# A mixture's first product as seven half-size products, its weights' sums streamed from DRAM

## The chip, the cores and the metric

One of the cores of a Trainium2 chip (trn2) runs the whole kernel. The metric is the device time of one execution in microseconds; lower is better. All data are fp32.

## The reference

A recurrence of attention kind (four batches, eight heads, 768 steps, head size 40) feeds a mixture of four experts:

```python
for t in range(S):
    y[:, :, t] = np.einsum('bhd,bhde->bhe', rt, state)
    Sa = np.einsum('bhde,bhe->bhd', state, at)
    state_decay = state * wt[:, :, None, :] - np.einsum('bhd,bhe->bhde', Sa, bt)
    state = state_decay + np.einsum('bhd,bhe->bhde', vt, kt)
x = y.transpose(0, 2, 1, 3).reshape(3072, 320)
p = domain_probs / (domain_probs.sum(-1, keepdims=True) + 1e-09)
for e in range(4):
    h = np.maximum(x @ w1[e], 0.0)            # 320 -> 1024
    out += p[:, e:e + 1] * (h @ w2[e])        # 1024 -> 320
```

## The kernel before, in words

**Units and chunks.** The 768 steps are cut into 12 chunks of 64. A unit is one chunk of two batches, 128 rows; there are 24 units, two to a chunk. The recurrence inside a unit is written in closed form: small products of 64x64 and 32x32 on PE (L371, L583, L595), a triangular system solved by substitution on POOL (L544, L557), and the state carried from unit to unit (L692, L693). The steps of a unit, by the names of their PSUM tiles: pg, pNT and pKT turn data; pc, pfe and pev are scores and their products (`within`); pY and pQ finish the triangular inverse (`merge`); prn, psat, pxr and pdy are the recurrent step (`step`). On DVE, ET and SX are masked copies (L382) of pfe and pxr; G is a running product (L401); `blocks` and M (L516, L519) prepare the substitution. pdy needs SX. Its result Y goes by twelve DMAs (L711) into xT, the transposed input of the mixture.

**The mixture.** From the second chunk on both units of a chunk go through the mixture together: 256 tokens, 320 inputs in two groups of 128 rows and a last one of 64. `up` (L718) makes one half of an expert's hidden layer from a piece of w1: 8 matmuls of 128 rows by 256 tokens (L734), and the last 64 inputs as 4 matmuls that take turns in the two halves of the array's rows (L726). Each fp32 matmul shows as two instructions in the trace. The result lies in two PSUM banks of the tag `mm`, which has three, and ACT writes relu of it to SBUF (L739). The second product, h times w2, is already done as seven half-size products for each expert: sums of w2 are made once (`add_weights`), sums of h by DVE after each expert (`add_h`, L835), and the products (L841) in `down_1` and `down_2`. DVE adds them into the output with the gates (L750, L752). The down products of an expert are issued while the next one's up products are.

**Order.** The main loop (L1021) runs the generators of three units side by side and calls `gap` four times for each unit; a gap puts two parts of the mixture (`mix`) onto the queues. The framework's scheduler may still move instructions within what dependences allow, except where `keep_in_program_order` pins them. Each engine then works through its compiled list. w1 is loaded anew for each chunk, in pieces of 512 KB and two times 64 KB (L282), into two buffers; a new load goes out when the piece before the last has been used (`used`). SP issues these loads, the loads of the next units (natW, natB, natK, natV at L184, the raw forms at L205), xT (L711) and the output (L757) from one queue. V is copied from natV into VC by ACT (L462).

Of the kernel before, what the change touches and what calls it, by code (L numbers as in the profile page):

```python
# [7 lines left out]
FP32 = mybir.dt.float32  # L8
I32 = mybir.dt.int32
ALU = mybir.AluOpType  # L10
ACTF = mybir.ActivationFunctionType
# [4 lines left out]
def kernel(  # L16
# [35 lines left out]

    nc = tc.nc

    B, H, S, D = r.shape
    E, DM, F = moe_w1.shape
    P = 128
    L = 64  # L60
    Q = 32
    NC = S // L
# [5 lines left out]
    const = ctx.enter_context(tc.tile_pool(name="const", bufs=1))  # L68
    sb = ctx.enter_context(tc.tile_pool(name="sb", bufs=1))
    ps = ctx.enter_context(tc.tile_pool(name="ps", bufs=1, space=bass.MemoryType.PSUM))  # L70

    def big(name):
        return ps.tile([P, 512], FP32, name=name, tag="big", bufs=5)
# [6 lines left out]
        base=0, channel_multiplier=-1,  # L80
    )

    upf = sb.tile([P, L], FP32, name="upf", tag="s", bufs=3)
    diagf = sb.tile([P, Q], FP32, name="diagf", tag="s", bufs=3)
    for t, n, op in ((upf, L, ALU.is_gt), (diagf, Q, ALU.is_equal)):
        nc.vector.memset(t[:], 1.0)
        for q in range(P // n):
# [26 lines left out]
    def set_pick():  # L114
        nc.gpsimd.memset(pick, 0.0)
        for n, (g, j) in enumerate(PLACES):
            for s in range(2):
                for c in (0, DT) if g == 2 else (0,):
                    w_ = DT if g == 2 else P
                    o = pick[64 * s:64 * s + D, n, c:c + w_]  # L120
                    nc.gpsimd.affine_select(
                        out=o, in_=o, pattern=[[-1, w_]], compare_op=ALU.not_equal, fill=1.0,
                        base=(2 * j + s) * D - g * P, channel_multiplier=1,
                    )

    first = const.tile([P, 2 * NJ, L], FP32, name="first")
    nc.gpsimd.memset(first[:], 0.0)
# [51 lines left out]

    def load(q, names):  # L180
        for x in names:
            q.n[x] = t = sb.tile([P, H, D], FP32, name=f"nat{x}", tag=f"nat{x}", bufs=2 if x in "WV" else 1)
            for i, bb in enumerate(q.b):
                nc.sync.dma_start(  # L184
                    out=t[i * L:(i + 1) * L], in_=srcs[x][bb, :, q.c * L:(q.c + 1) * L, :].rearrange("h t e -> t h e"),
                )
# [27 lines left out]
    def part(i):  # L214
        return slice(i * L, (i + 1) * L)
# [39 lines left out]
    class Piece:  # L255
        pass

    n_pieces = 2 * E * (1 + NC)
    pieces = []

    in_sums = {k + 5 * x: k - 1 for x in range(3) for k in (1, 2, 3)}
# [1 line left out]
    def load_piece():  # L263

        k = len(pieces)
        e, x = k // 2 % E, k % 2
        if k in in_sums:
            t = sums[in_sums[k]]
        else:
            t = sb.tile([P, PIECE], FP32, name="w1p", tag="w1p", bufs=2)  # L270
        q = Piece()
        q.main = t[:, 0:2 * HF * P].rearrange("p (g c) -> p g c", g=2)
        q.last = t[:, 2 * HF * P:PIECE].rearrange("p (f c) -> p f c", c=P)
        cols = slice(x * HF * P, (x + 1) * HF * P)
        moves = [(q.main, moe_w1[e, 0:2 * P, cols].rearrange("(g p) c -> p g c", p=P))]
        for i in range(2):
            half_cols = slice((2 * x + i) * HF // 2 * P, (2 * x + i + 1) * HF // 2 * P)
            moves.append(
                (q.last[i * DT:(i + 1) * DT], moe_w1[e, 2 * P:DM, half_cols].rearrange("d (f c) -> d f c", c=P))
            )  # L280
        for to, src in moves:
            tc.keep_in_program_order(nc.sync.dma_start(out=to, in_=src))  # L282
        pieces.append(q)

    def used(n):

        while len(pieces) < n_pieces:
            k = len(pieces)
            if k in in_sums:
                before = k - 5 if k >= 5 else -1  # L290
            else:
                at = [x for x in range(k) if x not in in_sums]
                before = at[-2] if len(at) > 1 else -1
            if before >= n:
                break
            load_piece()

    def load_w2(e):
        tc.keep_in_program_order(nc.sync.dma_start(out=w2_sb[e][:], in_=moe_w2[e].rearrange("(f p) d -> p f d", p=P)))
# [84 lines left out]
    def within(q):  # L384
# [24 lines left out]
        yield  # L409

        pg = by(turn("pg", tok(Gv), q.u == 2)[:], 64)[:, :, 0:D]
        gp = sb.tile([P, H, D], FP32, name="gp")
        pin(nc.vector.tensor_tensor(out=gp[:], in0=pg, in1=n["W"][:], op=ALU.mult))
        pin(nc.vector.reciprocal(out=gp[:], in_=gp[:]))  # L414

# [20 lines left out]
            nc.scalar.copy(out=t[:].rearrange("p j t -> p (j t)"), in_=turn("p" + name, tok(x), q.u == 1)[:])  # L436
            return t

        def token_V():
            return n["paddedV"][:, :, 0:D] if q.u < PADDED else n["V"][:]  # L440

        def causal_scores(VT):
            pc = quadrants(banks("pc"), 0, BY_TOKENS, L, lambda j, s, i: (
                d_half(j, s), i, j, of_slots(VT, d_half(j, s), j, i, D), of_slots(q.RT, d_half(j, s), j, i, D),
# [13 lines left out]
        ins = nc.vector.tensor_tensor(out=at_ij, in0=at_ij, in1=Gv.rearrange("p (j i) t -> p i j t", i=2), op=ALU.mult)  # L458
        pin(ins)
        q.VC = VCs()  # L460
        if q.u > 0:
            nc.scalar.copy(out=q.VC[:, :, 0:D], in_=token_V())  # L462
        if q.u >= PADDED:
            VT = turn_rv()
        yield
# [28 lines left out]
        yield  # L494

        if q.u == 0:
            tc.keep_in_program_order(nc.scalar.copy(out=q.VC[:, :, 0:D], in_=token_V()))
        q.EV = EVs()
        pev = quadrants(banks("pev"), 0, BY_TOKENS, D, lambda j, s, i: (
            i, i ^ s, j, ET[half(i), head(j, s), :], q.VC[half(i), head(j, s), 0:D],  # L500
# [9 lines left out]

    def substitute(q, eng, between=None):

        blocks = sb.tile([P, H, Q], FP32, name="blocks")
        for i in range(P // Q):
            move = nc.scalar.copy if i >= 2 else nc.vector.tensor_copy
            tc.keep_in_program_order(move(out=blocks[quarter(i)], in_=q.F[quarter(i), :, quarter(i % 2)]))  # L516
# [7 lines left out]
        on_diag = M[:].rearrange("p c r -> p (c r)")[:, Q + 1::2 * (Q + 1)]  # L524
        tc.keep_in_program_order(nc.vector.memset(on_diag, 0.0))

        Z = sb.tile([P, 4, Q // 4, Q], FP32, name="Z")
        q.Z = Z[:, 0]
        by_second = Z[:, 1:3].rearrange("p x k r -> p (x k) r")
        below = M[:].rearrange("p c r -> p (c r)")[:, 1::2 * (Q + 1)]  # L530
# [32 lines left out]
    def merge(q):  # L563


        Qc = sb.tile([P, H, Q], FP32, name="Qc", tag="q", bufs=2)
        QTc = sb.tile([P, H, Q], FP32, name="QTc", tag="q", bufs=2)
        tc.keep_in_program_order(nc.vector.transpose(out=dealt(Qc[:]), in_=q.Z))
        tc.keep_in_program_order(
            nc.vector.transpose(  # L570
                out=QTc[:].rearrange("p h r -> p (h r)"), in_=Qc[:].rearrange("p h c -> p (h c)"),
            )
        )
        q.QT = QTs()
        for i in range(P // Q):
            ins = nc.gpsimd.tensor_copy(out=q.QT[quarter(i), :, quarter(i % 2)], in_=QTc[quarter(i)])  # L576
            tc.keep_in_program_order(ins)
        yield

        py = big("pY")  # L580
        for h in range(H):
            for i in (1, 3):
                nc.tensor.matmul(  # L583
                    out=py[quarter(i - 1), h * Q:(h + 1) * Q], lhsT=q.F[quarter(i), h, 0:Q],
                    rhs=QTc[quarter(i), h, :], start=True, stop=True,
                )
        Y = sb.tile([P, H, Q], FP32, name="Yq")
        for i in (0, 2):
            nc.scalar.copy(out=Y[quarter(i)].rearrange("p h t -> p (h t)"), in_=py[quarter(i), 0:H * Q])
        yield  # L590

        pq = big("pQ")
        for h in range(H):
            for i in (0, 2):
                nc.tensor.matmul(  # L595
                    out=pq[quarter(i), h * Q:(h + 1) * Q], lhsT=Qc[quarter(i), h, :],
                    rhs=Y[quarter(i), h, :], start=True, stop=True,
                )
        for i in (0, 2):
            nc.scalar.copy(out=q.QT[quarter(i), :, quarter(1)], in_=by(pq[quarter(i), 0:H * Q], Q))  # L600
        yield
# [116 lines left out]
    def up(k, xT, n, width):  # L718

        w1 = pieces[k]  # L720
        h = sb.tile([P, HF, 2 * P], FP32, name="hs", tag="hs", bufs=3)
        ph = [ps.tile([P, HF // 2, n], FP32, name="ph", tag="mm", bufs=3) for _ in range(2)]

        for f in range(HF // 2):
# [90 lines left out]
    def mixture_of_chunk(qs, xT):  # L815

        hs, a_sums, osb = {}, {}, []
        at = 2 * E * (qs[0].c + 1)

        def ups(e, x):  # L820
            hs[e, x] = up(at + 2 * e + x, xT, 2 * P, P)
            used(at + 2 * e + x + 1)

        def of_h(e, s, x):
            return hs[e, x][:, :, s * P:(s + 1) * P]

        def add_h(e):
            a = {(s, x): of_h(e, s, x) for s in range(2) for x in range(2)}
            for n, x, y, op in (
                (1, a[0, 0], a[1, 1], ALU.add), (7, a[0, 1], a[1, 1], ALU.subtract),  # L830
                (5, a[0, 0], a[0, 1], ALU.add), (2, a[1, 0], a[1, 1], ALU.add),
                (6, a[1, 0], a[0, 0], ALU.subtract),
            ):
                t = a_sums[e, n] = sb.tile([P, HF, P], FP32, name=f"a{n}")
                nc.vector.tensor_tensor(out=t[:], in0=x, in1=y, op=op)  # L835
# [49 lines left out]


        before = last[:]
        for e in range(E):
            todo.append(lambda e=e: ups(e, 0))
            if before:  # L890
                todo.append(before[0])
                todo.append(lambda e=e: ups(e, 1))
                todo.append(lambda e=e, then=before[1]: (then(), add_h(e)))
            else:
                todo.append(lambda e=e: (ups(e, 1), add_h(e)))
            second = down_2_at_end if (qs[0].end and e == E - 1) else down_2
            before = [lambda e=e: down_1(e), lambda e=e, second=second: second(e)]
        last[:] = before
# [104 lines left out]
    run(m)  # L1003
    run(s, 2)
    run(ws[2], 1)
    load(units[3], "WBKV")
    go(load_raw(units[3], "AVR"))
    mix(1)
    run(ws[2], 3)
# [11 lines left out]
    for u in range(1, NU):  # L1021
# [32 lines left out]

        if u + 3 < NU:
            go(load_raw(begin(u + 3), "WA"))
            load(units[u + 3], "WBKV")
            later.extend(load_raw(units[u + 3], "VR"))
        run(w, 2)
        if early:  # L1060
# [58 lines left out]
```

## Time and profile before

| | |
|---|---|
| runs | 1143.93 and 1148.85 us, median 1146.39 |
| profiled execution | 1141.15 us, its span 1139.1 us |
| granted TensorE clock, mean | 0.988 |
| one unit in the steady part | 43.6 us |
| busy DVE, 600 to 700 us | 72.71 us |
| DMA read and written | 111.79 and 3.93 MB |

Rows of the timeline read: start, length, engine, line, operation, output <- inputs, shapes (array rows x columns, then partitions x elements), how many instructions are merged, and in brackets the idle time before and what ended it. [...] the distance between starts tells the pace.

### The profile page before, as it was taken

How to read it: one execution, taken by the hardware profiler on the slowest of the kernel's cores; microseconds unless marked ns; L12 is line 12 of the kernel's file. 1: busy time of each engine (PE TensorE's matmuls, PEld its weight loads, DVE VectorE, ACT ScalarE, POOL GpSimd, SP SyncE). 2: the span in 40 equal slices, each digit the busy share in tenths (PEclk: the TensorE clock that was granted, in tenths of full speed). 3: DMA queues.
4: the chain of work that ended last, by engine and by line, in shares of the span. 5: the costliest groups of instructions: out<-in, count | busy, mean ns of one | idle time of the engine just before them, and what ended most of it. 6: DMA issues, size and time to landing. Idle time of an engine off the chain costs nothing.

```text
span 1139.1 us, 38245 instructions
## 1 busy us (share of the span) xinstructions
PE 1099.4 (97%) x16036; PEld 976.6 (86%) x16036; DVE 757.8 (67%) x1553; ACT 338.0 (30%) x860; POOL 473.6 (42%) x1221
## 2 busy tenths in 40 slices
PE   6899997999999999999999999999999999999998
PEld 5777776888998989889899898888989898888887
DVE  8756647697767768667677677677677586553343
ACT  2333333333233232332332332332332322311110
POOL 4005626662724635625526526437337246340000
PEclk8899998999999999999999999999999999999999
DMA  7784643254263454444453453443543442231330
GB/s 118 213 245 124 131 99 78 65 132 101 76 146 89 107 128 100 119 122 101 115 121 83 123 118 86 118 102 84 139 102 87 117 110 64 75 90 55 105 92 12
DMA packets 268867, 122.16 MB, mean 107 GB/s; under 512 B 213737, under 2 KB 242073, under 8 KB 268697
## 3 DMA queue, kind: packets, MB, share of 16 engines
q1 hardware_dynamic: 265416, 119.12, 42.7%
q8 instruction: 126, 2.06, 0.8%
q10 hardware_dynamic: 3280, 0.61, 0.3%
q14 instruction: 45, 0.36, 0.1%
HBM read 111.79 MB, written 3.93 MB: 102 GB/s over the span
## 4 chain that ended last, share of the span: by engine, by line
PE 87%; DVE 4%; SPq 2%; DMA 2%; POOL 2%; ACT 2%; issue 1%; DVEq 0%; ACTq 0%
PE ph L734 29%; PE p L841 28%; PE ph L726 9%; PE pdy L371 4%; PE pfe L371 2%; PE psat L371 2%; PE pxr L371 2%; PE prn L371 2%; PE po L775 2%; PE pQ L595 1%; PE pc L371 1%; PE pY L583 1%; PE pev L371 1%; POOL Z L557 1%; PE pg L335 1%
## 5 line engine op out<-in xcount | busy, mean ns | idle before, releaser
L734 PE MATMUL ph<-xT,w1p 128*128 128x256 f32 (+1 forms) x1520 | 344.1, 379 | 2.2 <-issue 2.2
L734 PEld LDWEIGHTS ph<-xT,w1p 128*128 128x128 f32 x1520 | 274.3, 190 | 65.1 <-issue 27.3
L544 POOL TENSOR_TENSOR Z<-M,Z 128x62 f32<-128x62 f32 (+7 forms) x352 | 143.3, 407 | 368.6 <-DVE M L535 336.0
L557 POOL TENSOR_TENSOR Z<-Z 128x31 f32<-128x31 f32 (+7 forms) x704 | 257.2, 365 | 55.2
L835 DVE TENSOR_TENSOR a<-hs 128x512 f32<-128x512 f32 x220 | 152.4, 710 | 128.2 <-ACT hs L739 128.2
L739 ACT ACTIVATE hs<-ph 128x512 f32<-128x512 f32 (+1 forms) x208 | 115.7, 564 | 295.5 <-PE ph L734 295.1
L841 PE MATMUL p<-sums,a 128*128 128x160 f32 x1056 | 165.1, 299 | 0.0
L752 DVE SCALAR_TENSOR_TENSOR osb<-p,gate,osb 128x320 f32<-128x320 f32 (+1 forms) x243 | 107.9, 481 | 74.9 <-PE p L841 70.9
L841 PEld LDWEIGHTS p<-sums,a 128*128 128x128 f32 x1056 | 152.9, 190 | 2.3
L726 PE MATMUL ph<-xT,w1p 64*128 64x256 f32 (+1 forms) x760 | 110.1, 398 | 1.2 <-issue 1.1
L841 PE MATMUL p<-w,hs 128*128 128x160 f32 x704 | 102.9, 299 | 0.0
L841 PE MATMUL p<-w,a 128*128 128x160 f32 x704 | 102.8, 299 | 0.0
L841 PEld LDWEIGHTS p<-w,hs 128*128 128x128 f32 x704 | 100.3, 190 | 2.2
L841 PEld LDWEIGHTS p<-w,a 128*128 128x128 f32 x704 | 98.0, 190 | 0.0
L576 POOL COPY QT<-QTc 32x256 f32<-32x256 f32 x96 | 51.6, 537 | 111.5 <-DVE QTc L570 103.7
L726 PEld LDWEIGHTS ph<-xT,w1p 64*128 64x128 f32 x760 | 67.8, 187 | 14.4 <-issue 4.4
L519 DVE STREAM_TRANSPOSE M<-blocks 128x1024 f32<-128x1024 f32 x24 | 47.0, 1957 | 23.1 <-ACT blocks L516 23.0
L414 DVE RECIPROCAL gp<-gp 128x320 f32<-128x320 f32 x24 | 51.7, 2152 | 0.8
L504 ACT COPY EV<-pev 64x160 f32<-64x160 f32 x96 | 23.4, 286 | 66.8 <-PE pev L371 66.3
L371 PE MATMUL pdy<-VC,k_tok 64*64 64x104 f32 (+1 forms) x768 | 41.6, 260 | 0.1
L600 ACT COPY QT<-pQ 32x256 f32<-32x256 f32 x48 | 17.4, 362 | 79.3 <-PE pQ L595 78.8
L626 ACT COPY SN<-prn 128x256 f32<-128x256 f32 x44 | 15.7, 370 | 84.1 <-DVE RH L621 81.9
(148 smaller groups left out, 1364.0 us busy)
## 6 DMA issues: line engine op xcount, KB each, us to landing
w1p<-in_moe_w_dram SPq DMA_DIRECT2D x95, 512.0 KB
w1p<-in_moe_w_dram SPq DMA_DIRECT2D x190, 64.0 KB
w<-in_moe_w_dram SPq DMA_DIRECT2D x4, 1280.0 KB
sums<-in_moe_w_dram SPq DMA_DIRECT2D x9, 512.0 KB
natW<-in_w_dram SPq DMA_DIRECT2D x48, 80.0 KB
natB<-in_b_dram SPq DMA_DIRECT2D x48, 80.0 KB
natK<-in_k_dram SPq DMA_DIRECT2D x48, 80.0 KB
out_dram<-osb SPq DMA_DIRECT2D x46, 80.0 KB
```

Of the source, the lines that this page charges most:

```text
L371: nc.tensor.matmul(out=p[row][half(col), lo + at * out_cols:lo + (at + 1) * out_cols], lhsT=lhsT, rhs=rhs, start=(n == 0), stop=(n == len( ...
L414: pin(nc.vector.reciprocal(out=gp[:], in_=gp[:]))
L519: ins = nc.vector.transpose(out=M[:], in_=cols)
L544: ins = eng.tensor_tensor(out=Z[:, 1:3, 0:n, j + 1:Q], in0=M[:, j:j + 2, None, j + 1:Q].to_broadcast([P, 2, n, m]), in1=Z[:, here, 0:n, j: ...
L557: eng.tensor_tensor(out=z[:, 0], in0=z[:, 0], in1=z[:, x], op=ALU.add)
L576: ins = nc.gpsimd.tensor_copy(out=q.QT[quarter(i), :, quarter(i % 2)], in_=QTc[quarter(i)])
L726: nc.tensor.matmul(out=ph[i][:, f, :], lhsT=w1.last[i * DT:(i + 1) * DT, f, :], rhs=xT[i * DT:(i + 1) * DT, 2, :], start=(f == 0), stop=False,
L734: nc.tensor.matmul(out=ph[i][:, f, :], lhsT=w1.main[:, g, at * P:(at + 1) * P], rhs=xT[:, g, :], start=False, stop=(g == 1 and f == HF // ...
L739: nc.scalar.activation(out=h[:, i * HF // 2:(i + 1) * HF // 2, 0:n], in_=ph[i][:], func=ACTF.Relu,)
L752: nc.vector.scalar_tensor_tensor(out=to, in0=p, scalar=sc, in1=to, op0=ALU.mult, op1=ALU.add)
L835: nc.vector.tensor_tensor(out=t[:], in0=x, in1=y, op=op)
L841: nc.tensor.matmul(out=p[:, n * HD:(n + 1) * HD], lhsT=a[:, f, :], rhs=b[:, f, :], start=(f == 0), stop=(f == HF - 1),)
```

## The change

From the fourth chunk on the first product is done as seven half-size products too. Tokens are split in halves s, the two row groups of x are g, and the hidden columns in two halves f. Four sums of w1 for each expert (s1 to s4) are made by DVE in the third chunk, while its pieces lie in SBUF, and written to DRAM (`sum_w1`). From then on the weights arrive as quarters of 256 KB in a ring of seven, eight for each expert: three quarters of w1 itself, its last 64 rows, and the four sums, in the order a00, s2, s1, a01, last rows, s3, a11, s4 (`PER_EXPERT`). Each is loaded when the one seven places before it has been used. Three products start their banks and four add onto what lies there; between them ACT copies a bank out (p1, c01, c10, c11) and PE then adds the next product onto the same bank. DVE makes c01, c10 and c11 whole with five sums of 512 elements for each expert, and five sums of x for each chunk (`sum_x`). An expert's up work is now `ups_1` (five products and the last rows) and `ups_2` (two products and the last rows), in the places of the two `ups` before.

To make room: V goes by DMA straight into VC from the fourth unit on, gp is written in place of natW, Z has three parts on POOL's way, Yq shares a buffer with `blocks`, hidden tiles and the w1 buffers are fixed places. In the first chunks the piece buffers lie in the ring; in the third, both pieces of an expert are loaded only after `sum_w1`.

```diff
+    PER_EXPERT = ((0, 0), 1, 0, (0, 1), None, 2, (1, 1), 3)
+    def sum_w1(e, k):
+        a00, a01, a10, a11 = (p.main[:, g, :] for p in pieces[k:k + 2] for g in range(2))
+        s1, s3 = spare[:, 0:QUARTER], spare[:, QUARTER:2 * QUARTER]
+        for n, to, x, y, op in (
+            (0, s1, a10, a11, ALU.add), (2, s3, a00, a10, ALU.subtract),
+            (1, a00, s1, a00, ALU.subtract), (3, a01, a01, a00, ALU.subtract),
+        ):
+            nc.vector.tensor_tensor(out=to, in0=x, in1=y, op=op)
+            tc.keep_in_program_order(nc.sync.dma_start(out=w1_sums[e][n], in_=to))
...
+        def product(p, w, x, start=False, stop=False):
+            for f in range(HF):
+                nc.tensor.matmul(
+                    out=p[:, f, :], lhsT=w[:, f, :], rhs=x, start=(start and f == 0), stop=(stop and f == HF - 1),
+                    skip_group_check=True,
+                )
+        def last_rows(w, low, high):
+            for f in range(HF):
+                for i, (p, x, stop) in enumerate((low, high)):
+                    rows = slice(i * DT, (i + 1) * DT)
+                    nc.tensor.matmul(
+                        out=p[:, f, :], lhsT=w[rows, f, :], rhs=x[rows], start=False, stop=(stop and f == HF - 1),
+                        skip_group_check=True,
+                    )
...
+        def ups_1(e):
...
+            product(x, a00, of_x(0, 0), True)
+            nc.scalar.copy(out=p1[:], in_=x[:])
+            load_quarters(k + N_RING + 1)
+            product(w, s2, t2, True)
+            nc.scalar.copy(out=c01, in_=w[:])
+            load_quarters(k + N_RING + 2)
+            product(z, s1, t1, True)
+            nc.scalar.copy(out=c10, in_=z[:])
+            load_quarters(k + N_RING + 3)
+            product(x, a01, of_x(1, 0))
+            load_quarters(k + N_RING + 4)
+            last_rows(rows, (x, of_x(2, 0), True), (w, of_x(2, 1), False))
+            relu(c00, x[:])
+            product(w, s3, of_x(0, 1))
+            nc.scalar.copy(out=c11, in_=w[:])
+            plus(c01, c01, p1[:])
+            plus(c11, c11, c10)
+            plus(c11, c11, p1[:])
+            relu(c11, c11)
+        def ups_2(e):
...
+            product(w, a11, t4)
+            last_rows(rows, (z, of_x(2, 1), False), (w, of_x(2, 0), True))
+            plus(c10, w[:], p1[:])
+            relu(c10, c10)
+            product(z, s4, of_x(1, 1), stop=True)
+            plus(c01, z[:], c01)
+            relu(c01, c01)
+            load_quarters(k + N_RING + 8)
...
-            todo.append(lambda e=e: ups(e, 0))
+            todo.append(lambda e=e: ups_1(e) if split else ups(e, 0))
-                todo.append(lambda e=e: ups(e, 1))
+                todo.append(lambda e=e: ups_2(e) if split else ups(e, 1))
...
-            nc.scalar.copy(out=q.VC[:, :, 0:D], in_=token_V())
+        if q.u >= PADDED:
+            for i, bb in enumerate(q.b):
+                src = srcs["V"][bb, :, q.c * L:(q.c + 1) * L, :].rearrange("h t e -> t h e")
+                nc.sync.dma_start(out=q.VC[part(i), :, 0:D], in_=src)
```

## The prediction

> **What bounds the kernel now.** I read the page first (parts 1 and 4), then PE's groups by form, then the timelines of PE, DVE and SP over one unit.
>
> ```profile
> PE 1099.4 (97%) x16036; PEld 976.6 (86%) x16036; DVE 757.8 (67%) x1553; ACT 338.0 (30%) x860; POOL 473.6 (42%) x1221
> ...
> PE 87%; DVE 4%; SPq 2%; DMA 2%; POOL 2%; ACT 2%; issue 1%; DVEq 0%; ACTq 0%
> ```
>
> PE is the chain: 97% busy, 87% of it. So PE time removed is time won, if nothing new makes PE wait. DVE is the next fullest, 71 to 73% in each 100 us stretch from 300 to 800. A unit (two of a chunk's four experts) takes 43.6 us (pg starts at 605.62 and 649.29). Its PE order, from the end of one recurrence step to the next pg:
>
> ```profile
> 627.98 0.69 PE L595 MATMUL pQ<-Yq,Qc 32*32 32x32 f32 x32
> ...
> 630.67 1.26 PE L726 MATMUL ph<-xT,w1p 64*128 64x256 f32 x8
> 631.86 3.72 PE L734 MATMUL ph<-xT,w1p 128*128 128x256 f32 x16
> 635.41 2.34 PE L841 MATMUL p<-w,hs 128*128 128x160 f32 x16
> 637.59 1.25 PE L841 MATMUL p<-sums,a 128*128 128x160 f32 x8
> 638.77 0.68 PE L371 MATMUL pev<-VC,ET 64*64 64x40 f32 x32
> 639.25 0.67 PE L371 MATMUL pxr<-RT,SaT 64*64 64x64 f32 x32
> ...
> 640.33 1.13 PE L726 MATMUL ph<-xT,w1p 64*128 64x256 f32 x8
> 641.39 3.72 PE L734 MATMUL ph<-xT,w1p 128*128 128x256 f32 x16
> 644.95 1.25 PE L841 MATMUL p<-sums,a 128*128 128x160 f32 x8
> ...
> 649.29 0.60 PE L335 MATMUL pg<-ident,G 128*128 128x128 f32 x4
> ```
>
> Between psat (ends 630.67) and pev lie 8.1 us of mixture, between pxr and pg another 9 us. That is cover for what the other engines do for the recurrence. DVE in the same stretch:
>
> ```profile
> 629.15 0.38 DVE L752 SCALAR_TENSOR_TENSOR osb<-p,minus_gate,osb 128x160 f32<-128x160 f32 x1
> ...
> 633.29 1.96 DVE L519 STREAM_TRANSPOSE M<-blocks 128x1024 f32<-128x1024 f32 x1 [1.69 <-ACT blocks L516]
> ...
> 640.43 0.77 DVE L382 COPY_PREDICATED SX<-mask_up,pxr 128x256 f32<-128x256 int32 x2
> ```
>
> SX, which pdy needs, is ready at 641.2; PE takes pdy up only after 649.3. Eight us of slack.
>
> [...] DVE's starts follow the compiled order. [...] the row of L835 has a median of 684. [...]
>
> **The change, part by part** (durations from one execution with a span of 1139.1 us, its own time 1141.15; the median of the runs is 1146.39, 7.3 above the span).
>
> *PE work.* Before, a piece runs from 618.91 to 623.54, 4.63 us; two per expert, 9.26. After: 28 products of 128 columns, two passes each, 56 instructions, and two bursts of 8 row pairs. 128-wide costs are in the first unit:
>
> ```profile
> 130.13 1.61 PE L734 MATMUL ph<-xT,w1p 128*128 128x128 f32 x13 [1.11 <-issue]
> ...
> 143.14 0.72 PE L726 MATMUL ph<-xT,sums 64*128 64x128 f32 x8
> 143.79 2.05 PE L734 MATMUL ph<-xT,sums 128*128 128x128 f32 x16
> 145.77 0.71 PE L726 MATMUL ph<-xT,sums 64*128 64x128 f32 x8
> ```
>
> The first row gives the pace inside a stream: (1.61 - 0.275)/12 = 0.111; I take 0.112. The group at 143.79 takes 1.98 for 16, so entering and leaving a row burst adds 1.98 - 16x0.112 = 0.19. Four pairs take 0.65, eight 0.65 + 4x0.112 = 1.10, with the 0.19 1.29. Per expert 56x0.112 + 2x1.29 = 8.85. Saved 0.41; nine chunks of four experts, 36 times: **-14.8 us**. The arithmetic falls by an eighth of the main part; halving the width gives most of it back (256 columns cost 3.56/16 = 0.223, not 2x0.112, but the row bursts double). If the pace were 0.124 throughout, 56x0.124 + 2.58 = 9.52 and the change would cost PE 9 us.
>
> *DVE and ACT.* Per expert three sums from SBUF and two from PSUM, 5x0.69; per chunk five small ones. Per unit 6.9 + 0.6: DVE goes from about 31 to 39 us of 43. ACT gets about four more 0.6 us steps per expert at 30% load. Neither is a bound by its sum; the order is.
>
> *Order, the decisive part.* The compiled order of the changed kernel puts only the first three products of an expert (a00, s2, s1) between psat and pev, and then pev, pxr, pg and pdy at once, with the remaining products after them. This holds for 13 units (e2, e4 to e26 of the 36 experts). PE after psat: 24x0.112 = 2.68, pev 0.48, pxr 1.08, pg 0.45, pdy's first few 0.1: at SX after 4.8 us. DVE meanwhile has queued between the last add of down_2 and SX: G's transposes, gl, memset and scan (0.73 + 0.19 + 0.07 + 1.32), blocks 0.57, ET 0.90, gl 0.18, M 1.96 + 0.1, one new sum 0.69, AT 0.70 + 0.69, Z and M 0.69 each, memset 0.07, SX 0.77: 10.3 us. In the trace DVE ends that last add 1.1 us before psat ends (629.53 against 630.67). SX is ready 10.3 - 1.1 = 9.2 us after psat; PE waits 4.4. 13 units: **+57 us**. Before, G's transposes and scan stood in another phase and p431's adds were all that was extra. Behind the waiting pdy stand all later products, so nothing covers it. Bounds: 3 us (DVE starts earlier, short gaps overlap), 6 us (M also waits for ACT's blocks, as the 1.69 above).
>
> *Waits on banks.* All three mm banks are held across ups_1 and ups_2. p75 goes into the bank that plus(c10) must read: rows end, then 0.3 drain and wake, 0.69, 0.1 back, against 1.0 of s4: about even. But DVE has p431's four adds (1.6) and a1 (0.7) ahead, so I take 0.2 per expert, 36 times: **+7** (0 to 25). p431 behind relu(c00) and a01 behind the copy of p1 have 0.9 and 1.8 us of products as cover: nothing; without it 0.7 each.
>
> *Quarters.* Per expert 9 DMAs for 6, 2 MB for 1.25; engines were busy 0.42 to 0.47, so bandwidth is no bound. SP issues in order:
>
> ```profile
> 611.33 9.05 SPq L711 DMA_DIRECT2D xT<-Y  x12
> 620.49 1.66 SPq L282 DMA_DIRECT2D w1p<-in_moe_w_dram  x3
> ```
>
> s4 of odd experts stands behind twelve xT issues (9 us) and V into VC (1.3), both after pdy. Where part of pdy is put after down_2 (7 units) s4 leaves 11.8 us after it [...] **+6** (0 to 20). Elsewhere Y is ready some 13 us earlier: nothing.
>
> *Chunk 2 and V.* Sixteen sums (11 us of DVE) and 4 MB written before the next expert's piece may land: DVE 2.8, write 4 to 6, reload 4, against about 5 to 12 us of other PE work. I take **+8** (0 to 20). V by DMA instead of an ACT copy takes ACT's waits on pdy away and gives them to SP, where the ring's 7 quarters cover them; gp in place, Z of three parts and Yq sharing blocks: nothing, their readers end before; each would cost a DVE wait under 1 us.
>
> Sum: 1139.1 - 14.8 + 57 + 7 + 6 + 8 = 1202; on the median's footing 1202 + 7 = 1209, and I say **1208 us**.
>
> **The rivals.** (1) *The wait for SX decides* (forecast), own range 1180 to 1240. For it: the order, and DVE's rows. (2) *The stream becomes the bound*: SP issues some 32 us per 43.6 us unit (xT 8.6, w1p 6.4, the rest mostly 0.43 and 0.63 each), with six more 35; s1 of the next expert waits in SP for a01, which now comes after pdy, and raw loads queue behind. At 3 us more in each of 18 units: 1209 + 54 = 1263. Against it: SP had 10 us per unit to spare and seven quarters are ahead. (3) *Not slower*: DVE's work before SX is covered. It decides where the wait is under (23 + 15 - 21)/13 = 1.3 us with the other waits, 2.9 without them. Then -14.8 plus 0 to 21 gives 1131 to 1153. For it: DVE's idle gaps (1.69, 2.02, 2.82 us in the stretch) show room. Against: the ones before SX lie ahead of work that stays queued.
>
> **How the numbers follow.** (1) 0.63, (2) 0.16, (3) 0.16, 0.05 for the rest. Under 2% (23 us) a measurement of this kernel can't tell from no change: 1123 to 1169. Faster needs 23 us where PE saves 15: 0.03. Same 0.15, slower 0.82. The range runs from 1160 to 1260: it leaves out most of (3) and the upper half of (2).
>
> **What would show it.** Right: PE idle before pdy, released by DVE's SX, about 4 us in 13 units; units of 47 to 48 us; L916 matmuls 112 ns apart; DVE near 80%. Wrong: pdy starting at once (3); PE or PEld waiting for ring by DMA as the largest item (2); a chunk 2 that is longer by over 20 us.

## The result, and the profile after

The changed kernel took 1254.33 and 1257.16 us, median 1255.74, against 1146.39: a ratio of 1.0954, 95% interval 1.084 to 1.1068. It is slower by 109 us, inside the stated range but 48 us above the stated time. The profiled execution is the one of 1257.16 us, with a span of 1255.4.

Parts 1 and 4 of the page of the changed kernel, the rows that answer to those shown of before:

```profile
PE 1152.4 (92%) x17476; PEld 1056.1 (84%) x17476; DVE 891.6 (71%) x1794; ACT 414.1 (33%) x983; POOL 492.5 (39%) x1221
...
PE 70%; DVE 11%; DMA 7%; SPq 4%; issue 3%; ACT 2%; POOL 2%; DVEq 0%; ACTq 0%; POOLq 0%
```

PE falls from 97 to 92% busy, and yet its busy time *grows*, from 1099.4 to 1152.4 us, with less arithmetic. DVE's share of the chain goes from 4 to 11%, and DMA's and SP's from 4 to 11% together. The view of the cores, before and then after, has the reason for the growth:

```profile
core 0: 1139.1 us, clock 0.988
```

```profile
core 0: 1255.4 us, clock 0.952
```

In both traces the granted clock is recorded as 1.00 or 0.50 only. A mean of 0.952 is about 2 x 0.048 x 1255 = 120 us at half clock, against 27 before. So two things came: PE's idle time rose from 33.9 to 96.9 us, and half clock took up to (120 - 27)/2 = 46 us. Together that is 109 of the span's 116.

Where PE waits, from the view of the waits, PE alone (total, times, longest):

```profile
PE pdy L425 <- DVE SX L436: 32.4, 14, 3.1
PE pu L916 <- DMA ring<-w_sums: 22.3, 11, 3.0
PE pev L425 <- DVE ET L436: 9.6, 4, 5.8
PE pQ L653 <- ACT Yq L647: 8.0, 5, 3.1
```

The first two rows are the new ones: SX for pdy, and a late quarter of weights. One unit shows both the wait and what follows it. PE, from its timeline (pdy's later rows left out):

```profile
693.03 1.95 PE L916 MATMUL pu<-tx,ring 128*128 128x128 f32 x16
694.91 0.68 PE L425 MATMUL pev<-VC,ET 64*64 64x40 f32 x32
...
697.06 0.47 PE L425 MATMUL pdy<-VC,k_tok 64*64 64x104 f32 x4
700.11 0.43 PE L425 MATMUL pdy<-SX,n_tok 64*64 64x104 f32 x1 [2.58 <-DVE SX L436]
...
703.06 2.07 PE L916 MATMUL pu<-xT,ring 128*128 128x128 f32 x8
...
712.85 1.05 PE L916 MATMUL pu<-tx,ring 128*128 128x128 f32 x8
```

After the wait, eight instructions of a product take 2.07 us, with a granted clock of 0.50 (703 to 706 us); ten microseconds later eight of the same shape take 1.05, at 1.00 (712 to 715 us). DVE in the same stretch, from its timeline:

```profile
694.68 2.04 DVE L574 STREAM_TRANSPOSE M<-blocks 128x1024 f32<-128x1024 f32 x1
696.61 0.68 DVE L935 TENSOR_TENSOR h<-h,p 128x512 f32<-128x512 f32 x1
...
698.98 0.72 DVE L593 TENSOR_TENSOR M<-M,Z 128x512 f32<-128x512 f32 x1
699.58 0.81 DVE L436 COPY_PREDICATED SX<-mask_up,pxr 128x256 f32<-128x256 int32 x2
```

DVE isn't idle there: it works down its list, and SX is the last of it. The quarter's lateness stands in SP's timeline, and PE's wait in PE's:

```profile
521.99 8.89 SPq L769 DMA_DIRECT2D xT<-Y  x12
530.99 1.42 SPq L515 DMA_DIRECT2D VC<-in_v_dram  x2
532.50 0.56 SPq L338 DMA_DIRECT2D ring<-w_sums  x1
```

```profile
535.53 1.16 PE L916 MATMUL pu<-xT,ring 128*128 128x128 f32 x8 [1.65 <-DMA ring<-w_sums]
```

s4's load is issued 10.5 us after the first of the twelve moves into xT, and PE starts on it 3.0 us after its issue.

### The profile page after: what moved, and what is told of

The parts are those of the page before. It is cut to its first block, busy times and chain, and to the rows that moved or that the text cites. A ratio compares the mean times of both kernels' runs of the same rounds, so it can differ in the third digit from the quotient of the medians.

```text
span 1255.4 us, 41999 instructions
## 1 busy us (share of the span) xinstructions
PE 1152.4 (92%) x17476; PEld 1056.1 (84%) x17476; DVE 891.6 (71%) x1794; ACT 414.1 (33%) x983; POOL 492.5 (39%) x1221
## 4 chain that ended last, share of the span: by engine, by line
PE 70%; DVE 11%; DMA 7%; SPq 4%; issue 3%; ACT 2%; POOL 2%; DVEq 0%; ACTq 0%; POOLq 0%
PE p L1008 24%; PE pu L916 17%; PE ph L792 6%; PE pu L926 6%; PE pdy L425 4%; DMA ring<-w_sums 3%; SPq L769 2%; DVE M L574 2%; PE ph L784 2%; PE po L833 2%; DMA ring<-in_moe_w_dram 2%; PE pfe L425 1%; PE prn L425 1%; PE pc L425 1%; PE psat L425 1%
## 5 line engine op out<-in xcount | busy, mean ns | idle before, releaser
L916 PE MATMUL pu<-xT,ring 128*128 128x128 f32 x1152 | 172.1, 294 | 23.6 <-DMA ring<-w_sums 22.3
L916 PEld LDWEIGHTS pu<-xT,ring 128*128 128x128 f32 x1152 | 147.4, 200 | 38.8 <-DMA ring<-w_sums 25.1
L1002 DVE TENSOR_TENSOR a<-h,h 128x512 f32<-128x512 f32 x168 | 115.6, 690 | 34.0 <-ACT h L797 18.9
L916 PE MATMUL pu<-tx,ring 128*128 128x128 f32 x864 | 110.7, 278 | 0.0
L916 PEld LDWEIGHTS pu<-tx,ring 128*128 128x128 f32 x864 | 103.1, 192 | 1.1 <-issue 0.2
L1008 PE MATMUL p<-w,h 128*128 128x160 f32 x704 | 103.2, 300 | 0.0
L1008 PEld LDWEIGHTS p<-w,h 128*128 128x128 f32 x704 | 97.6, 190 | 0.4
L935 DVE TENSOR_TENSOR h<-h,h 128x512 f32<-128x512 f32 x36 | 25.8, 716 | 94.5 <-ACT h L969 94.5
L926 PE MATMUL pu<-xT,ring 64*128 64x128 f32 x1152 | 92.8, 288 | 0.0
L425 PE MATMUL pdy<-SX,n_tok 64*64 64x104 f32 (+1 forms) x768 | 60.7, 300 | 32.4 <-DVE SX L436 32.4
L926 PEld LDWEIGHTS pu<-xT,ring 64*128 64x128 f32 x1152 | 78.7, 190 | 9.0 <-issue 0.4
L792 PE MATMUL ph<-xT,ring 128*128 128x256 f32 (+1 forms) x368 | 80.4, 373 | 0.0
```

What stands on the lines that cost most here:

```text
L425: nc.tensor.matmul(out=p[row][half(col), lo + at * out_cols:lo + (at + 1) * out_cols], lhsT=lhsT, rhs=rhs, start=(n == 0), stop=(n == len( ...
L792: nc.tensor.matmul(out=ph[i][:, f, :], lhsT=w1.main[:, g, at * P:(at + 1) * P], rhs=xT[:, g, :], start=False, stop=(g == 1 and f == HF // ...
L916: nc.tensor.matmul(out=p[:, f, :], lhsT=w[:, f, :], rhs=x, start=(start and f == 0), stop=(stop and f == HF - 1), skip_group_check=True,)
L926: nc.tensor.matmul(out=p[:, f, :], lhsT=w[rows, f, :], rhs=x[rows], start=False, stop=(stop and f == HF - 1), skip_group_check=True,)
L935: nc.vector.tensor_tensor(out=to, in0=x, in1=y, op=ALU.add)
L1008: nc.tensor.matmul(out=p[:, n * HD:(n + 1) * HD], lhsT=a[:, f, :], rhs=b[:, f, :], start=(f == 0), stop=(f == HF - 1),)
```

## The experiments

The first theory was that of the prediction: PE's order leaves SX uncovered. The trace added that each wait also costs clock. The rival was the stream of quarters. Times are medians; the kernel before measured 1141.9 to 1146.7 us beside them.

**PE's order put back.** Order edges without a wait hold pev behind s3, and pdy behind s4:

```diff
+    def behind_ups(ins):
+        tc.add_manual_dep(ins.ins, last_up[0], nosync, reason="behind_ups")
...
+                if behind and last_up[0] is not None:
+                    behind_ups(ins)
```

> The changed kernel, computing the same; only PE's order is held: pev not before the third sum's product (s3) of the expert's first part, pdy not before s4, so that products lie between psat and pev and between pxr and pdy again, as in the kernel before. Theory A (PE waits for SX because pdy comes at once, and each wait of some 2.5 us also halves the clock for 3.4 us or more): the 32 us of pdy waiting for SX fall under 5, the 121 us of half clock fall to 50 or less, the time falls by 50 to 75 us to 1180 to 1205. Theory B (the stream of quarters is the bound): the waits of the products for the ring grow by what the SX waits lose, the time stays above 1235.

1230.2 us, ratio 1.0779 (1.0743 to 1.0815). The waits for SX went, as theory A said, but another came:

```profile
PE prn L433 <- ACT NT L500: 24.2, 14, 3.0
...
PE pdy L433 <- DVE SX L446: 1.9, 3, 0.9
```

In ACT's timeline a relu waits (4.3 us in one unit) for DVE's sum, and the copy of NT, which prn needs, stands behind it. The time lies between the theories: a hole in the order was moved, not closed. The granted clock was 0.961.

**The same without loads.**

```diff
-            for to, src in moves:
+            for to, src in moves if k < N_RING else ():
```

> The same held order, and of the quarters only the first seven are loaded: the later products read what lies in the ring, so w1's data is left out from then on. No load of weights stands in SP's queue or is waited for after the third chunk. Theory A: the products' waits for the ring (22 us in the changed kernel) and their share of half clock go, 10 to 25 us below the kernel with the held order. Theory B: 50 us or more below it. If neither the stream nor SX is what is left, the difference is under 5 us.

1318.7 us, against every expectation. The scheduler had ordered the engines anew, and PE waited 86.5 us, ten times and up to 12.7, for DVE's h. It tells nothing of the stream; it tells that in this kernel an edit is only readable with the order held. The later experiments (but not the two that follow) therefore hold each engine's compiled list by such edges, instruction by instruction.

**The order alone, in the kernel before.** The gap with the second up and down parts goes behind pdy:

```diff
         run(s, 1)
-        gap(0)
...
         run(s)
+        if not early:
+            gap(0)
```

> The kernel before, computing the same; from the sixth unit on the second up and down parts of an expert are put behind pdy instead of between pxr and pdy, so pev, pxr, pg and pdy follow each other as in the changed kernel. No seven products, no sums of w1, no ring. Theory A (the order alone makes the loss): pdy waits for SX 1 to 3 us in most units, half clock rises from 30 us to 60 or more, the time rises by 25 to 60 us to 1170 to 1205. Rival (without the five new sums on DVE SX is in time): no wait over 0.5 us, the time within 10 us of 1146.

1195.4 us, ratio 1.0466 (1.0443 to 1.0488): 53 us lost without a single new product or load. The time fits theory A, its mechanism only in small part:

```profile
PE pc L371 <- DVE RT L223: 12.2, 9, 2.2
PE pdy L371 <- DVE SX L382: 7.0, 13, 1.5
```

Half clock rose only from 27 to 39 us (clock 0.984), which is some 6 us of time, and idle PE by 20 us. The rest lies in instructions that start further apart: row pairs of ph take 18 us more in all and pdy 9; in places pieces of ph stand inside pdy, but what makes up the 27 us isn't settled. So the place alone can cost 53 us, but this run doesn't show that the wait for SX is what costs them; the run with SX early does that.

**Filled with work.**

```diff
+        for _ in range(10 if q.u > 8 else 0):
+            ins = nc.tensor.matmul(out=p[0][:, 0:P], lhsT=ident[:], rhs=ident[:], start=True, stop=True)
+            tc.keep_in_program_order(ins)
```

> The kernel with pdy early of the run before this one, and from the tenth unit on ten products of 128x128 with the identity (20 instructions, 2.2 us), written into pdy's bank ahead of pdy and overwritten by it, so PE works where it waited. Theory A with the clock (an idle PE gets half the clock): half clock falls back to 30 to 45 us and the time is 10 to 30 us below the run without these products, though work is added. Rival (the clock has nothing to do with the wait): no less half clock, the time the same or up to 30 us more.

1205.8 us, 10 above the run before it, clock 0.977 in the profiled execution and 0.984 in the other, so no better than before: what the rival wanted. But none of the waits for SX there was longer than 1.5 us, and half clock followed 1 of 91 waits that short in these traces (last section), so it can't decide on the clock. The next but one does.

**Only the stream taken away**, with all orders of the changed kernel held (the edit is that of the loads above):

> The changed kernel with the order of every engine held as it was compiled there, and of the quarters only the first seven loaded (w1's data is left out from then on; the products read what lies in the ring). So nothing but the stream goes. Theory A (the order costs, the stream a little): the products' waits for the ring (22 us in 11 waits) and half clock behind the longer ones go, 20 to 35 us below the changed kernel, 1220 to 1235, with the waits for SX as they were. Theory B (the stream is the bound): below 1195. Theory C (the ring's waits only take the place of others): 1250 or more.

1237.8 us, ratio 1.0816 (1.0766 to 1.0866), 18 below the changed kernel. No wait for a quarter is left on PE's list; SX's grew from 32.4 us in 14 to this:

```profile
PE pdy L425 <- DVE SX L436: 35.9, 16, 3.1
```

So the stream isn't the bound (theory B wanted under 1195), and it isn't free.

**Work in the hole**, orders held:

```diff
+        for _ in range(10 if q.u > 10 and q.u != 20 else 0):
+            ins = nc.tensor.matmul(out=p[0][:, 0:P], lhsT=ident[:], rhs=ident[:], start=True, stop=True)
```

> The changed kernel with all orders held, computing the same, and in 12 late units ten products with the identity (20 instructions, 2.2 us at full clock) written into pdy's bank ahead of pdy, which overwrites them: PE works on nothing useful where it waited for SX. If the idle PE loses the clock: half clock falls from 121 us to 85 or less, and the time is 10 to 25 us below the changed kernel, 1230 to 1245, though 26 us of work is added. Rival (half clock has another cause, data or load): half clock stays over 110, the time is within 6 us of 1256 or above it.

1251.4 us, 4 below the changed kernel, which for the time is what the rival wanted: a difference within the intervals (ratios to the kernel before of 1.0935, 1.0886 to 1.0985, and 1.0954); the clock rises from 0.952 to 0.969, half clock falls from 120 to 78 us. A unit of it, PE's timeline:

```profile
601.87 2.48 PE L735 MATMUL pdy<-ident 128*128 128x128 f32 x20
...
606.71 1.16 PE L924 MATMUL pu<-xT,ring 128*128 128x128 f32 x8
```

The product behind pdy takes 1.16 where it took 2.07. The waits for SX fall from 32.4 to 12.7 us, and the stream of quarters is the same. The clock is answered: it is the idle PE that loses it. The gain in time is less than expected, and may be nothing: the added work takes back what the clock gives.

**SX first on DVE**, orders held, 13 units. In DVE's list, where h is the new sum of L935:

```diff
 h<-h,p
+SX<-mask_up,pxr  x2
 M memset; AT<-rawA; Z<-M; AT<-AT,G; M<-M,Z
-SX<-mask_up,pxr  x2
```

> The changed kernel, computing the same, orders held, with one edit on DVE in 13 units: SX's two copies stand right behind the addition before M's memset, ahead of that memset, Z, M's addition and AT's two steps (2.3 to 2.9 us). Theory A (SX late on DVE makes the waits and the half clock): pdy's waits for SX fall from 32 us to 12 or less, half clock to 85 us or less, the time to 1205 to 1225. Rival (another wait takes its place, as it did when PE's order was held): the waits move to M's or AT's readers, the time stays above 1240.

1219.9 us, ratio 1.0675 (1.062 to 1.073): 36 us by the medians, some 32 by the ratios, from the place of two instructions. Waits of PE:

```profile
PE pu L916 <- DMA ring<-w_sums: 20.0, 9, 4.1
...
PE pdy L425 <- DVE SX L436: 5.9, 7, 1.0
```

The clock is 0.972, and no reader of M or AT took the wait over; the only new wait of any size is prn's for NT, 3.9 us in 2.

**And s4 ahead of xT on SP**, in 14 units: its load moves from behind the two of V to before the twelve of xT, the rest of SP's list kept.

> As the run before it (SX early on DVE), and on SP the load of s4 of the expert that stood behind the twelve moves into xT and the two of V goes ahead of them, in 14 units. Computes the same. Theory A: the products' waits for the ring (22 us, 11 times in the changed kernel) fall under 5 us, half clock with them, 15 to 30 us below the run with SX early alone: 1180 to 1205. Rival (hidden or replaced): within 6 us of the run with SX early alone.

1193.7 us, ratio 1.0434 (1.0379 to 1.0489): 26 us more. The clock is 0.979.

```profile
PE pdy L425 <- DVE SX L436: 6.6, 8, 1.0
...
PE pu L916 <- DMA ring<-w_sums: 3.7, 2, 2.7
```

The two edits win back 62 of the 109 us (some 60 by the ratios). That is the best version found; it doesn't reach the kernel before.

**What the width costs.** In the kernel before, orders held, arithmetic whole:

```diff
+        parts = (slice(0, P), slice(P, n)) if k >= 4 * 2 * E else (slice(0, n),)
...
+                    for part_ in parts:
...
-                        rhs=xT[:, g, :], start=False, stop=(g == 1 and f == HF // 2 - 1),
+                            out=ph[i][:, f, part_], lhsT=w1.main[:, g, at * P:(at + 1) * P], rhs=xT[:, g, part_],
```

> The kernel before, computing the same, every engine's order held; from the fourth chunk on each product of w1 with 256 tokens is issued as two of 128, so the arithmetic stays whole and only the width is halved: per expert 64 instructions of 128 columns for 32 of 256, and row bursts of eight pairs for four. From the pace in the traces (0.112 against 0.216 in a stream, two bursts 0.1 longer each): 64 x 0.112 = 7.2 against 7.1 plus 0.2, so 0.3 us more per expert, 11 us in 36: 1150 to 1162. Seven eighths of the main part would then take 0.9 us off each expert, 32 us in all, if nothing else were lost; the changed kernel measured 0.1 more than before instead, so 0.7 per expert would be the entries into the shorter groups. Rival (width costs nothing): 1146 within 4 us. Rival (narrow products themselves are the loss): 1170 or more.

1176.3 us, ratio 1.0244 (1.0187 to 1.0302), 30 above the kernel before, so above the expectation: the time is what the second rival wanted. The trace divides it: units without a wait took 44.27 us for 43.55, so 0.36 per expert and 13 us in 36, close to what was expected. The rest are new waits (14 us more idle PE) with half clock behind some of them (20 us more, which costs 10), in units that took up to 48.6:

```profile
PE psat L371 <- issue: 10.1, 6, 2.6
PE ph L728 <- issue: 8.4, 7, 2.2
```

A list made for another pace fits this, but no run with a list of its own shows it.

**The third chunk.** First without the sums, then with the reload as in other chunks too:

```diff
-            nc.vector.tensor_tensor(out=to, in0=x, in1=y, op=op)
-            tc.keep_in_program_order(nc.sync.dma_start(out=w1_sums[e][n], in_=to))
...
-                moves = [(t, w1_sums[e][what])]
+                moves = [(t, moe_w1[e, 0:P, 0:QUARTER])]
```

> The kernel with SX and s4 early, all orders held, and in the third chunk no sums of w1: the sixteen additions on DVE and the sixteen writes to DRAM are left out, and later, in place of each sum, a quarter of w1 of the same size is loaded, so the products from the fourth chunk on read other numbers at the same pace. Forecast of record: the sums cost 8 us (0 to 20); the trace of the changed kernel shows 5 us of PE waiting for the ring's pieces in the third chunk, 2.6 us for ET behind the additions, and 5 us lost to half clock around them. If these are the sums' doing: 8 to 16 us below that kernel, 1178 to 1186. Rival (hidden, the waits come from SP and remain): within 4 us of 1194.

1194.7 us for 1193.7, as the rival had it: the sums and their writes cost nothing that can be measured. The wait of ph for a piece stayed, 4.75 us.

```diff
-            if c != SUM_CHUNK:
-                used(at + 2 * e + x + 1)
-            elif x:
-                sum_w1(e, at + 2 * e)
-                used(at + 2 * e + 2)
...
+            used(at + 2 * e + x + 1)
```

> As the run without sums, sums left out in the same way, and in the third chunk each piece of w1 is loaded again as soon as the piece before the last is used, as in the other chunks, instead of both pieces of an expert after its second; SP's order is the scheduler's, the other engines' orders are held. If the late reload is what the third chunk costs: the wait of ph for a piece (4.8 us) and the half clock behind it go, the time falls 5 to 12 us under 1194. Rival (the third chunk's loss lies elsewhere, in PE's order): within 4 us of 1194.

1196.3 us: no gain. The wait for the piece went, and pev's longest wait for ET in that place grew from 2.6 to 6.8 us. The twelfth unit's pg still came 4 us sooner (435.06 for 439.17), and was overtaken later: SP's list wasn't held, and the waits for quarters grew, from 5.9 us in 4 to 8.6 in 6.

## Why the prediction was right, and where it was wrong

The direction was right, and so was the step named as decisive: PE waits for SX, because DVE reaches it last. The sum was not. The result lies 48 us above the stated time and 4 us below the end of the range, and that it lies inside is in part luck: the saving on PE and the waits on banks came to nearly nothing, the quarters and the first chunks cost several times what was put down for them, and the loss of clock, up to 46 us, stands in no term.

**PE work, -14.8: wrong.** In a unit of the changed kernel without half clock the up work of two experts took 18.74 us for 18.49 before (start to start, idle left out): 9.37 per expert, where 8.85 was forecast. With both order edits an undisturbed unit gave 9.19, so 2 us saved in 36 experts. The pace of 0.112 was right (the 2016 instructions of L916, two to a product, start 112 ns apart inside a stream; the median length of one is 275 ns), and a burst nearly so (1.17 from its first start to the next product's, with 0.19 more in the products on its two sides; 1.10 and 0.19 were taken). The term that failed is the entries, counted only at the two bursts. Behind psat, pY, pdy or a row burst the second instruction of a product starts 213 ns after its first, not 112, and that happens 3.6 times per expert; the last instruction ahead of a burst is 0.09 longer. So the products' row is 6.84 us per expert, 0.57 above 56 x 0.112. Of the 0.34 that the forecast lacks, about half are the entries behind psat, pY and pdy, half the bursts. Halving the width cost 0.36 per expert by itself (in a stream 256 columns take 0.216, not the 0.223 of the prediction, which holds a burst's side), and the eighth that is left out won 9.61 - 9.19 = 0.42, not the 0.9 that was estimated ahead of the run on the width.

**The order, +57: right in place and cause, wrong in size.** Forecast were 13 units and 4.4 us each; measured 14 waits of 2.3 us. DVE's list from G's transposes to the end of SX took 9.6 us (690.81 to 700.39), not 10.3, and PE reached SX's first reader about 0.7 us later than estimated. Against this, the loss of clock behind the waits is missing from the sum; with it, the edit that moves SX alone is worth 32 to 36 us, and 5.9 us of waits are left. Of the signs named, units of 47 to 48 us were forecast, and from the twelfth to the last but one they took 47.1 to 56.7.

**Banks, +7: wrong.** No product of the down parts waits for a bank in the view of the waits; that term is nothing in this order. Its 0.3 us from PE to DVE and 0.1 back are near the trace of before: DVE's L752 started 0.34 us after the start of the last product it waited for (median of 38 waits), PE 0.08 to 0.15 us after the end of a DVE result (four waits). In the run without loads and with the order free it is just this wait, of p for DVE's h, that took 86.5 us, while DVE stood still for POOL.

**Quarters, +6: right in place, too small.** s4 behind twelve moves into xT, and V, is what the trace shows, but in both kinds of units, 22.3 us in 11 waits. Moving it wins 26 us, clock included. Taking the whole stream away won 18 while SX's waits were left in. The +6 rested on an estimate of a quarter's landing that no view of the kernel before shows. In the trace of the changed kernel the weight loads of PE that waited for a quarter began 2.7 to 4.7 us after its issue, median 3.0, in 13 waits.

**Third chunk, +8, and side edits at nothing: too small, and in part for another reason.** Up to the twelfth unit's pg the changed kernel is 15 us later (446.26 for 431.26) and has done less of the mixture by then: four of the seven products and the last rows of one expert's up, and one expert's downs, some 6.4 + 7.7 us, which stand in the tail. So 29 us are lost there. 11 of them are idle PE, and half clock (61 us for 27) takes about 17, so nearly all. The sums are not it (1194.7 us without them for 1193.7), though SP waited once for the writes of an expert's sums, 3.3 us: the load behind them was issued 6.3 us after the first write (344.70 for 338.37). The wait for the late reload (4.2 us; the reload is issued at 310.23 and in use at 314.36) is in it, but without that reload it gave way to one for ET, and nothing was won. Another part is a side edit that was put at under 1 us: Yq in the buffer of `blocks`. Its copy on ACT waits for DVE's M, pQ waits up to 3.1 us for the copy, and the seventh unit takes 43.2 us for 36.4 before. A buffer of its own for Yq wasn't tried, for want of room in SBUF, so this part is read from the trace alone. The sign that the prediction named, a third chunk longer by over 20 us, doesn't decide: from the first product of the third chunk's mixture to that of the fourth's lie 109.4 us for 87.8, but some 12 of the 21.6 more are down products and steps of the recurrence that now fall into this stretch.

**The balance.** Up to the twelfth unit's pg 29, the next twelve units 81.6, tail 19.7 - 14.1 = 5.6: 116, the difference of the spans. In those twelve units idle PE is 45 us more and half clock 55 us, so some 27; the remaining 10 are pdy taken up in pieces and the slightly longer up work.

The rivals: (2), the stream as the bound, gave 1263, nearest to the result, but for a cause that the held order without loads excludes. (3), SX covered, is out. What the forecast lacked as a whole is the clock. In the trace of the changed kernel it stands at 0.50 in stretches of 3.41 us (13 of the 21 whole ones) and of multiples of that, and waits of 2.5 us were enough (last section).

**Open.** Some 50 us lie between the best version and the kernel before: idle PE is 26 us more there, half clock some 12, up work 9 (465.4 for 456.7 us), the rest in pieces of pdy. They are mostly waits under 2 us; none was taken away singly.

## What to carry to other kernels

Where PE is full, ask of a rewritten product two things before its arithmetic: how often it is entered anew, and what its pieces used to cover. A step that needs another engine's result should have that result ahead of the mixture's work on that engine's list, and a load should not stand in a queue behind moves that wait for something later. An edit under a scheduler is priced only with the order held: here the same removal of loads gave 1318.7 us with the order free (beside PE's order put back) and 1237.8 with it held.

## What the runs showed of the hardware

- How long a wait must be to cost clock: over the thirteen traces, after the first 300 us, half clock followed (within 3.6 us of the wait's end) 1 of 91 idle stretches of PE of 0.7 to 1.5 us, 13 of 30 from 1.5 to 2, 12 of 17 from 2 to 2.5, and 67 of 71 of 2.5 and more (in the changed kernel's trace alone 14 of 16). So a wait of 2.5 us mostly costs up to 1.7 us again for each 3.41 us of half clock, and useless products in it cost no time that could be measured (1251.4 us for 1255.7).
- The idle share of a fixed step tells more in these traces than the wait's length. In each trace all stretches of half clock start on one grid of steps of 3.413 us, to within 1 ns. Of the steps after the first 300 us that began at full clock, half clock followed 68 of 68 in which PE was idle for 60% or more, 18 of 24 at 50 to 60%, 6 of 33 at 40 to 50%, and 1 of 3180 below. That fits what waits of 1.5 to 2.5 us did: they cost clock only sometimes, as they fell on the grid.
- Between products of 128 rows at 112 ns and row bursts (pairs of 64 rows, also at 112 ns) PE lost about 0.1 us on each side in the changed kernel: the last instruction before the change and the first (or first pair) after it took 202 to 213 ns.
